# First pair's 32x32 systems of a delta-rule attention relaid on VectorE instead of over DRAM, and weight loads issued from ScalarE's queue

## The chip, the cores and the metric

The kernel runs on one NeuronCore of a Trainium2 chip. Its engines are TensorE (PE; PEld is its weight load), VectorE (DVE), ScalarE (ACT), GpSimd (POOL) and SyncE (SP), which here only issues DMAs. Each engine works through its own instructions in program order and waits on semaphores. The metric is the device time of one execution in microseconds (us); the profiled execution gives the trace.

## The reference

The program computes three stages that feed each other. First a delta-rule attention over 4 batches x 8 heads, 768 steps, head size 48:

```
k_n = k / (norm(k) + 1e-6)
for t in range(S):
    y[:, :, t] = q_t @ state
    v_old = state^T k_t
    state = state + beta_t * outer(k_t, v_t - v_old)
```

Its output, as 3072 tokens x 384, goes through a first MoE layer, which has one expert with a rational activation: `h = x @ w_in` (384 -> 2048), `g = P(h) / Q(h)` with a cubic P and a quadratic Q, `g @ w_out` (2048 -> 384). That output goes through a second MoE: a gate, a greedy assignment of 3072 tokens to 8 experts of capacity 384 in the order of their logits, and per expert `relu(x @ w1) @ w2`. The weights `w_in` and `w_out` come as 64-bit floats and are decoded on the chip to 32-bit and split into two 16-bit halves.

## The kernel before, in words

The recurrence is rewritten in 12 chunks of 64 steps. For each chunk and each of its 32 heads a unit lower triangular 64x64 system, built from the Gram matrix of the chunk's keys, is inverted. It is cut into 2x2 blocks of 32x32; two chunks form a pair, so that a pair gives 128 systems of 32x32, one per partition. `gram_k` (L124) multiplies the keys on PE into PSUM (tile `tg`), copies them to SBUF (`ka`, L131) and writes them to DRAM (`dA`, L134). `subst` (L160) reads them back so that one system lies along one partition (L167, eight DMAs into `pmA`), scales them (L94 on ACT, L100 to L106 and L178 on DVE) and runs the substitution column by column. For the first pair it runs on DVE (L183, L184) and stops at 16x16 blocks (15 columns, flag `n16`); for the other pairs on POOL (L187, L188, 31 columns). The result `pmW` goes to DRAM (`dW`, L190) and is read back transposed: for the first pair by `inv_in` (L157), for others by `diag_in` (L202). For the first pair `parts` (L153, L154) also reads the off-diagonal blocks of the Gram matrix back from `dA`, and `merge` (L1109) joins the 16x16 inverses to 32x32 with two PE products (L148), a transposition (L1115) and a subtraction (L1118) per chunk. Then the blocks are joined to 64x64 (`comb` L216, `comb2` L229), and the chunk's update follows: `tr` (L250), `y` (L264), `ds` (L272). The chunk's output is rounded to two 16-bit halves (`xs`, L1375 on ACT and L1376 on DVE) and laid out for the MoE by six DMAs (`pack`, L1380, tile `xT`).

The first MoE takes eight units per chunk, 96 in all. A unit is 18 matmuls (`h`, L875), the rational function on ACT and DVE (L848 to L868), a split into halves (L840 on ACT, L841 on DVE or POOL), and 12 matmuls (L824).

Ahead of the first unit lies the prologue. It loads the weights (`w_in` in six loads of 1 MB, L317; `w_out` in sixteen of 384 KB, L325), decodes them on DVE (three instructions a piece, L312 to L314) and rounds them (L1133, L1134, L1137 on ACT, L1138 on DVE, L1135 on POOL). All these loads are issued by SP, in one queue with the attention's transfers. The pieces of `w_out` that are not needed at once are decoded between the units of the first chunk.

The order of the instructions is set ahead of time by a list scheduler (`Sched`, L405). It gives each task an engine and a place by estimated costs and by due weights, which stand in the table `PP` (L967) for the prologue and the first two chunks and in `LP` (L1010) for the loop over chunks 2 to 10; two more tables serve the last chunk and the second MoE. Where it sees PE idle in the prologue it puts in matmuls on zeros (`warm`, L1395), 542 of them in all, which keep PE active. DMAs take eight semaphores in turn, so each DMA waits until the one eight places before it has landed.

Of the kernel before, what the change touches and what calls it, by code (L numbers as in the profile page):

```python
# [22 lines left out]
class Att:  # L23
# [11 lines left out]
    def __init__(s,ctx,tc,q,k,v,beta,tg,rec):  # L35
# [114 lines left out]
    def parts(s,m,e,F,X):  # L150
        nc=s.nc; x=s.dA[m%2][e]
        for h in range(2):
            for b in range(2): o=64*h+32*b; nc.sync.dma_start(F[o+16:o+32,:,0:16],x[o+16:o+32,:,32*b:32*b+16])  # L153
            nc.sync.dma_start(X[64*h:64*h+32],x[64*h:64*h+32,:,32:64])  # L154
    def inv_in(s,m,e,D):
        for h in range(2):
            for b in range(2): o=64*h+32*b; s.nc.sync.dma_start(D[o:o+32],s.dW[m%2][h,b,e].rearrange("u j i -> j u i"))  # L157

    def subst(s,m,eng,n16=False):

        nc=s.nc; n=128; x={}; ss=s.ss[m%2]; z=[]
# [7 lines left out]
        z+=[lambda: load(0),lambda: load(1)]  # L169
# [20 lines left out]
        z.append(lambda: (nc.sync if n16 else nc.gpsimd).dma_start(s.dW[m%2].rearrange("h b c u j i -> (h b c u) (j i)"),x['W'][:,0:1024]))  # L190
# [94 lines left out]
class Moe:  # L285
# [35 lines left out]
    def dma_wo(s,f):  # L321
# [3 lines left out]
        s.nc.sync.dma_start(ti,s.w_out.bitcast(I32).rearrange("(f p) (d two) -> f p d two",p=128,two=2)[f])  # L325
# [1164 lines left out]
```

## Time and profile before

| | |
|---|---|
| time, median of 3 runs | 968.44 us (965.59 to 973.08) |
| the profiled execution's own time | 968.31 us, of which its span is 966.5 us |
| busy share of the span | PE 88%, DVE 80%, ACT 58%, POOL 42% |
| first MoE unit's first matmul (L875) | 110.69 us after the span's start |
| last MoE unit's first stage | 671.5 us |
| DMA traffic | 97.50 MB, mean 101 GB/s |

Times in rows are us from the span's start. The profile's page shows the span in 40 slices of 24.2 us; a digit is a busy share in tenths. In the chain of waits each piece is the work that released the next one.

### The profile page before, as it was taken

The numbers are of one execution on the slowest core, as the hardware profiler recorded it, in microseconds if no ns is written. First come the engines' busy times: TensorE is split into PE (matmuls) and PEld (weight loads), VectorE is DVE, ScalarE is ACT, GpSimd is POOL, SyncE is SP. The second block draws the span as 40 slices with busy tenths as digits, with TensorE's granted clock in tenths as the row PEclk, the third lists the DMA queues.
The fourth block names the chain that finished last, engine by engine and source line by source line (L and its number), as shares of the span: only waits on it lengthen the run. The fifth ranks groups of instructions, "written<-read, shape, count | busy, mean of one in ns | idle before, by whom it ended". The sixth has DMA issues, their size and how long they took to land.

```text
span 966.5 us, 30502 instructions
## 1 busy us (share of the span) xinstructions
PE 855.1 (88%) x12967; PEld 603.6 (62%) x12967; DVE 771.9 (80%) x1689; ACT 562.8 (58%) x1019; POOL 405.5 (42%) x596
## 2 busy tenths in 40 slices
PE   8967798698989997999899999986789889998996
PEld 6846576575767675767677666663565555555663
DVE  5654798887889988989898898876688988988930
ACT  2132477566778787888778787875226334443821
POOL 1025870785227853785587212201322304213611
PEclk9976899899999999999999999997899979999998
DMA  8886436220561153216141220100054305443700
GB/s 305 186 241 121 128 113 113 53 74 23 146 121 52 56 122 100 63 57 156 38 91 51 54 55 1 34 5 14 2 169 159 151 30 196 156 155 128 266 25 24
DMA packets 101512, 97.50 MB, mean 101 GB/s; under 512 B 78336, under 2 KB 86144, under 8 KB 98560
## 3 DMA queue, kind: packets, MB, share of 16 engines
q1 hardware_dynamic: 95280, 58.33, 24.3%
q0 software_dynamic: 6096, 37.23, 10.4%
q8 instruction: 101, 1.65, 0.8%
q14 instruction: 35, 0.29, 0.1%
HBM read 71.68 MB, written 18.87 MB: 94 GB/s over the span
## 4 chain that ended last, share of the span: by engine, by line
PE 32%; DVE 29%; ACT 11%; DMA 10%; issue 10%; POOL 4%; SPq 3%; POOLq 0%; DVEq 0%; ACTq 0%
PE ph L875 9%; PE eph L770 4%; PE px L824 4%; DVE q L864 3%; DVE w L867 3%; DVE w L868 3%; PE px L783 3%; PE px L1395 3%; DVE w L851 2%; ACT q L858 2%; DVE q L850 2%; DMA xg<-x2d,perm 2%; DVE w L852 2%; ACT w L861 2%; DMA w1f<-in_moe_w_dram,ix 2%
## 5 line engine op out<-in xcount | busy, mean ns | idle before, releaser
L875 PE MATMUL ph<-xT,wi 128*128 128x256 f16 x1656 | 202.7, 278 | 26.4 <-DVE w L851 24.1
L875 PEld LDWEIGHTS <-wi 128*128 128x128 f16 x1728 | 167.0, 100 | 71.5 <-DVE w L851 34.6
L824 PE MATMUL px<-wo,gg 128*128 128x392 f16 (+1 forms) x1116 | 203.5, 333 | 5.2 <-ACT gg L840 2.9
L824 PEld LDWEIGHTS <-gg 128*128 128x128 f16 x1116 | 106.4, 99 | 75.0 <-issue 5.0
L841 POOL TENSOR_TENSOR gg<-w,gg 128x512 f16<-128x512 f32 x59 | 70.5, 1194 | 181.8 <-ACT gg L840 139.4
L188 POOL TENSOR_TENSOR pmW<-pmW,pmT 128x31 f32<-128x31 f32 (+15 forms) x155 | 94.9, 612 | 11.1
L187 POOL TENSOR_TENSOR pmT<-pmW,pmA 128x31 f32<-128x31 f32 (+15 forms) x155 | 86.6, 559 | 11.4
L861 ACT ACTIVATE w<-ph,cf 128x512 f32<-128x512 f32 x88 | 68.2, 775 | 22.8 <-PE ph L875 20.3
L867 DVE TENSOR_TENSOR w<-w,ph 128x512 f32<-128x512 f32 x88 | 59.8, 681 | 22.4 <-ACT q L858 12.2
L852 DVE SCALAR_TENSOR_TENSOR w<-q,w 128x512 f32<-128x512 f32 x88 | 76.5, 869 | 1.3
L840 ACT ACTIVATE gg<-w 128x512 f16<-128x512 f32 x88 | 55.4, 630 | 37.8 <-DVE w L852 37.3
L864 DVE SCALAR_TENSOR_TENSOR q<-q,cf,ph 128x512 f32<-128x512 f32 x88 | 65.1, 740 | 12.4 <-ACT w L861 6.8
L858 ACT ACTIVATE q<-ph,cf 128x512 f32<-128x512 f32 x88 | 60.0, 682 | 23.3 <-PE ph L875 12.7
L783 PEld LDWEIGHTS <-rr 128*128 128x128 f16 x576 | 52.3, 97 | 33.6 <-issue 2.3
L868 DVE SCALAR_TENSOR_TENSOR w<-w,cf,ph 128x512 f32<-128x512 f32 x88 | 65.3, 742 | 9.9 <-ACT q L858 9.4
L1395 PEld LDWEIGHTS <-warm 128*128 128x128 f16 x542 | 54.1, 104 | 24.5 <-issue 10.5
L773 ACT ACTIVATE rr<-eph 128x384 f16<-128x384 f32 x64 | 31.0, 490 | 60.3 <-PE eph L770 52.4
L850 DVE SCALAR_TENSOR_TENSOR q<-q,ph 128x512 f32<-128x512 f32 x88 | 59.8, 680 | 6.9 <-ACT ph L849 6.4
L865 ACT ACTIVATE q<-q 128x512 f32<-128x512 f32 x88 | 55.2, 628 | 16.9 <-DVE q L864 15.9
L851 DVE SCALAR_TENSOR_TENSOR w<-w,cf,ph 128x512 f32<-128x512 f32 x88 | 65.0, 738 | 0.0
L848 ACT ACTIVATE ph<-q,cf 128x512 f32<-128x512 f32 x88 | 60.6, 688 | 6.4 <-DVE ss L103 2.8
L788 POOL DMA_INDIRECT out_dram<-yo,perm x24 | 28.1, 1170 | 81.9 <-ACT yo L785 75.0
(342 smaller groups left out, 1649.7 us busy)
## 6 DMA issues: line engine op xcount, KB each, us to landing
kt<-in_k_dram SPq DMA_DIRECT2D x12, 512.0 KB, 4.0
dA<-ka SPq DMA_DIRECT2D x11, 512.0 KB, 3.6
vn<-in_v_dram SPq DMA_DIRECT2D x12, 384.0 KB, 4.7
qt<-in_q_dram SPq DMA_DIRECT2D x24, 192.0 KB, 4.1
kn<-in_k_dram SPq DMA_DIRECT2D x12, 384.0 KB, 3.1
x2d<-xr SPq DMA_DIRECT2D x44, 96.0 KB, 2.4
xT<-xs SPq DMA_DIRECT2D x24, 144.0 KB, 3.0
wst<-in_moe_w_out_dram SPq DMA_DIRECT2D x8, 384.0 KB, 3.8
```

The costliest lines, as they stand in the source:

```text
L187: if half==0: eng.tensor_tensor(t,W[:,0:r,j:j+1].to_broadcast([n,r,k]),A[:,j:j+1,j+1:32].to_broadcast([n,r,k]),op=OP.mult)
L188: else: eng.tensor_tensor(W[:,0:r,j+1:32],W[:,0:r,j+1:32],t,op=OP.subtract)
L783: g.add(('PE',.163,lambda P=P,rh=rh,wh=wh,f=f,part=part,i=i: nc.tensor.matmul(P,r[:,rh,f,128*i:128*i+128],W2[:,wh,f],start=(f,part)==(0,0) ...
L824: te.matmul(T['px',un//8][bp][:,0:O.N],gg()[:,gh,i,128*bp:128*bp+128],M.wo[:,wh,fb,0:O.N],start=fb==0 and n==0,stop=fb==15 and n==2,skip_g ...
L851: add(('DVE',.07+.6*z,lambda: ve.scalar_tensor_tensor(w(),w(),cf[:,0:1],y(),op0=OP.add,op1=OP.mult)),W+Y,W,un+O.pd('w3',un))
L852: add(('DVE*',.07+.535*z,lambda: ve.scalar_tensor_tensor(w(),q(),2.0,w(),op0=OP.subtract,op1=OP.mult)),Q+W,W,un+O.pd('w4',un))
L861: ac.activation(w(),P(),AF.Identity,bias=cf[:,2:3],scale=cf[:,3:4])
L864: add(('DVE',.07+.6*z,lambda: ve.scalar_tensor_tensor(q(),q(),cf[:,4:5],P(),op0=OP.add,op1=OP.mult)),Q+Pn,Q,un+O.pd('mu',un))
L867: add(('DVE',.07+.535*z,lambda: ve.tensor_tensor(w(),w(),P(),op=OP.mult)),W+Pn,W,un+O.pd('w1',un))
L868: add(('DVE',.07+.6*z,lambda: ve.scalar_tensor_tensor(w(),w(),cf[:,1:2],P(),op0=OP.add,op1=OP.mult)),W+Pn,W,un+O.pd('w2',un))
L875: for wh,xh in ((0,0),(0,1),(1,0)): te.matmul(T['P',un][:,i],M.wi[:,wh,part,128*fb:128*fb+128],xT()[:,xh,part],start=n==0,stop=n==8); n+=1
L1395: for _ in range(n): nc.tensor.matmul((bk['px1'] if t is None else t)[:,0:256],warm[:,0:128],warm,start=True,stop=True)
```

## The change

The first pair no longer goes over DRAM. Its two Gram matrices are computed into two PSUM tiles (`rec` for chunk 1, `tg` for chunk 0). `gram_0` copies each in small pieces from PSUM: the four diagonal 32x32 blocks into one SBUF tile `G`, in an order in which one stream transposition on DVE (32x32 blocks) gives `pmA`; the off-diagonal 16-column blocks, masked by a constant `odd`, and the upper blocks straight into the tiles that `parts` filled. After the substitution a second stream transposition writes the inverses to a tile `nd`, where `inv_in` put them. So 31 DMAs on SP fall away (2 writes of `dA`, 8 reads into `pmA`, 12 of `parts`, 1 write of `dW`, 8 of `inv_in`). The 6 loads of `w_in` and 16 of `w_out` are issued by ACT's queue instead of SP's. All due weights in `PP` and `LP` are new, so the order of the prologue and of the loop is another one. In the instruction lists, the matmuls on zeros become 406, five of the 88 whole splits at L841 go from POOL to DVE, and two copies at L1202 from DVE to ACT. From the last chunk on, the order of each engine stays the same.

```diff
+        s.odd=c.tile([128,1],F32,name="odd"); nc.vector.tensor_reduce(s.odd,s.ident.rearrange("t (a b x) -> t a b x",b=2,x=16)[:,:,1],axis=AX.XY,op=OP.add)
...
+    def gram_0(s,c,P,F):
+        nc=s.nc; k=s.kT[c]; g=s.gram(k,k,0,s.rec if c else s.tg)
+        def out(i,act=True):
+            o=slice(32*i,32*i+32); b=32*(i%2); y=s.G.rearrange("t (x c p r) -> t c r p x",x=32,c=2,p=8)[o,c]; x=g[o,:,:,b:b+32]
+            if act: nc.scalar.activation(y,x,AF.Copy)
+            else: nc.vector.tensor_copy(y,x)
+        def off(i): o=slice(32*i,32*i+32); b=32*(i%2); nc.scalar.activation(F[o].rearrange("t (p r) x -> t r p x",r=2)[:,:,:,0:16],g[o,:,:,b:b+16],AF.Copy,scale=s.odd[o])
+        def top(h): o=slice(64*h,64*h+32); nc.scalar.activation(P[o].rearrange("t (p r) x -> t r p x",r=2),g[o,:,:,32:64],AF.Copy)
...
-    def parts(s,m,e,F,X):
-        nc=s.nc; x=s.dA[m%2][e]
...
-    def inv_in(s,m,e,D):
...
-    def subst(s,m,eng,n16=False):
+    def subst(s,m,eng,n16=False,D=None):
...
-        z+=[lambda: load(0),lambda: load(1)]
+        def sys():
+            load(None); nc.vector.transpose(x['A'][:,0:1024],s.G)
+        z+=[sys] if n16 else [lambda: load(0),lambda: load(1)]
...
-        z.append(lambda: (nc.sync if n16 else nc.gpsimd).dma_start(s.dW[m%2].rearrange("h b c u j i -> (h b c u) (j i)"),x['W'][:,0:1024]))
+        if n16: z.append(lambda: nc.vector.transpose(D.rearrange("p (n i) -> p i n",i=32),x['W'][:,0:1024].rearrange("p (j i) -> p i j",i=32)))
+        else: z.append(lambda: nc.gpsimd.dma_start(s.dW[m%2].rearrange("h b c u j i -> (h b c u) (j i)"),x['W'][:,0:1024]))
...
-        s.nc.sync.dma_start(ti,s.w_out.bitcast(I32).rearrange("(f p) (d two) -> f p d two",p=128,two=2)[f])
+        s.nc.scalar.dma_start(ti,s.w_out.bitcast(I32).rearrange("(f p) (d two) -> f p d two",p=128,two=2)[f])
...
-PP=dict(K=[7339.93,4085.14,1736.19,-2114.71,1742.45,2256.15,42.43,5191.74,-1312.5],
+PP=dict(K=[2081.9,2098.33,2116.11,2982.83,-3313.15,1372.22,2452.84,-1832.06,-2116.3],
...
+    def GK0(c):
+        x=CH[c]; f,pp=x['F'],x['P']; p=PW('gk',c); B_=RE if c else TG
+        add(('POOL',.7,lambda: po.memset(flat(f),0.0)),[],[f],PP['ms'])
+        b=mm(2.4,warm(lambda: A.gram_0(c,sl(pp),sl(f))),['rec' if c else 'tg'],[('kT',c)],B_,p,act=2800)
+        for i in range(4): ev(b,i,'AD',.55,B_,[('g0',c,i)]+['ka'][:c==i==0],p)
+        for i in range(4): ev(b,4+i,'ACT',.4,B_,[f],p+1)
+        for h in range(2): ev(b,8+h,'ACT',.55,B_,[pp],p+2)
...
-        add(('SP',(6,1.2),lambda: A.parts(0,c,sl(f),sl(pp))),[('dA',0,c)],[f,pp],p)
-        add(('SP',(4,1.2),lambda: A.inv_in(0,c,sl(d))),[('dW',0)],[d],p)
...
-        hf,j=divmod(k,3); add(('SP',(1,2.9),lambda: M.dma_wi(k,sp,wsi[k])),[],WS_(k),PP['wil'][k])
+        hf,j=divmod(k,3); add(('SP',(1,2.9),lambda: M.dma_wi(k,ac,wsi[k])),[],WS_(k),PP['wil'][k])
```

The order moves at three places that matter below. In the order's rows a line number of the changed kernel is its own. The first place is SP's queue behind the small loads, of the kernel before (`dA`, `pmA`, `ut`, `n` belong to the first pair, `wsi` and `wst` to the weights):

```order
L134 DMA dA_116<-ka 128x1024
L317 DMA wsi<-in_moe_w_in_dram 128x2048
L134 DMA dA_117<-xs 128x1024
L325 DMA wst<-in_moe_w_out_dram 128x768
L89 DMA vn_96<-in_v_dram 128x768
L92 DMA qt_94<-in_q_dram 48x1024 x2
L325 DMA wst<-in_moe_w_out_dram 128x768
L167 DMA pmA<-dA_116 16x32x32 x4
L167 DMA pmA<-dA_117 16x32x32 x4
L317 DMA wsi<-in_moe_w_in_dram 128x2048
```

and of the changed kernel, where `dA` and `pmA` already belong to the second pair:

```order
L86 DMA kt_90<-in_k_dram 128x1024
L88 DMA kn_92<-in_k_dram 128x768
L88 DMA kn_93<-in_k_dram 128x768
L90 DMA vn_97<-in_v_dram 128x768
L145 DMA dA_120<-ka 128x1024
L169 DMA pmA<-dA_120 16x32x32 x4
L145 DMA dA_121<-ka 128x1024
L169 DMA pmA<-dA_121 16x32x32 x4
```

The loads of inputs stand ahead of everything that waits for an engine, and no weight load stands between them.

The second place is DVE ahead of the first pair's substitution, in the changed kernel (`ka` is the tile `G`, `q` and `wof` are weights being decoded):

```order
L130 COPY ka<-tg 32x2x8x32 x2
L317 TENSOR_SCALAR q<-wo 128x512
L172 STREAM_TRANSPOSE pmA<-ka 128x1024
L318 SCALAR_TENSOR_TENSOR q<-wo,q 128x512
L317 TENSOR_SCALAR q<-wo 128x512
L319 SCALAR_TENSOR_TENSOR q<-wo,q 128x512
L318 SCALAR_TENSOR_TENSOR q<-wo,q 128x512
L101 TENSOR_TENSOR ss_103<-pmA,ss_103 128x32
L319 SCALAR_TENSOR_TENSOR q<-wo,q 128x512
L1151 SCALAR_TENSOR_TENSOR wi<-q,wi 128x512
L102 SCALAR_TENSOR_TENSOR ss_103<-ss_103 128x32
```

Before, L100 to L106 followed each other on DVE with nothing between them, behind ten decoding instructions; now decoding stands between the relaying, the scaling and the substitution.

The third place is ACT at the same time in the changed kernel (`n` and `ut` are the tiles of `merge`):

```order
L129 ACTIVATE ka<-rec 32x2x8x32 x2
L330 DMA wst<-in_moe_w_out_dram 128x768
L131 ACTIVATE n_207<-rec,odd 32x2x8x16
L132 ACTIVATE n_206<-rec 32x2x8x32
L1150 ACTIVATE wo<-wof 128x384
L330 DMA wst<-in_moe_w_out_dram 128x768
L129 ACTIVATE ka<-tg 32x2x8x32
L330 DMA gg<-in_moe_w_out_dram 128x768
L129 ACTIVATE ka<-tg 32x2x8x32
L131 ACTIVATE ut<-tg,odd 32x2x8x16
L330 DMA gg<-in_moe_w_out_dram 128x768
L132 ACTIVATE ut<-tg 32x2x8x32
```

Before, ACT issued no DMA and took one copy per Gram matrix (L131); now loads stand between the pieces that it copies, each behind its own wait.

## Rows read from the trace of the kernel before

**Rows 1.** The page: busy us and shares; DMA's busy tenths in 40 slices.
```profile
PE 855.1 (88%) x12967; PEld 603.6 (62%) x12967; DVE 771.9 (80%) x1689; ACT 562.8 (58%) x1019; POOL 405.5 (42%) x596
...
DMA  8886436220561153216141220100054305443700
```

**Rows 2.** Windows: stretch, busy us per engine, PE's granted clock, DMA share, GB/s.
```profile
0.00:12.00 12.00, 8.68 (x68) 6.32 (x69) 5.92 (x13) 1.49 (x2) 2.94 (x11) 1.00 0.85 325
12.00:36.00 24.00, 24.00 (x308) 20.72 (x308) 12.77 (x31) 7.98 (x15) 0.73 (x3) 1.00 0.92 230
...
49.40:104.00 54.60, 38.62 (x1197) 29.80 (x1198) 32.16 (x59) 18.05 (x30) 24.95 (x33) 0.72 0.70 180
...
110.70:204.00 93.30, 81.07 (x1615) 62.53 (x1613) 76.84 (x138) 61.90 (x112) 55.72 (x85) 0.93 0.38 87
204.00:390.00 186.00, 168.60 (x3187) 124.16 (x3186) 160.22 (x243) 138.72 (x234) 102.40 (x172) 0.99 0.36 87
...
671.00:966.50 295.50, 263.37 (x2127) 162.01 (x2126) 223.85 (x799) 118.23 (x266) 82.57 (x113) 0.95 0.33 120
```

**Rows 3.** Chain of waits, 0 to 140 us: start, us, what.
```profile
18.69 8.55 DMA vn<-in_v_dram
...
31.46 6.78 DMA wsi<-in_moe_w_in_dram
...
38.63 9.26 DMA wo<-in_moe_w_in_dram
...
48.28 6.12 DMA kt<-in_k_dram
```

**Rows 4.** Timeline, prologue: start, us, engine, line, operation, tiles [idle before, releaser].
```profile
11.23 0.46 PE L121 MATMUL tg<-kt 48*64 48x64 f32 x16
...
16.66 29.98 PE L1395 MATMUL px<-warm 128*128 128x256 f16 x273
...
21.90 9.46 SPq L167 DMA_DIRECT2D pmA<-dA  x8
...
36.04 0.21 DVE L100 TENSOR_TENSOR ss<-pmA,ss 128x32 f32<-128x32 f32 x1 [7.01 <-ACT ss L94]
...
49.18 0.21 DVE L184 TENSOR_TENSOR pmW<-pmW,pmT 128x30 f32<-128x30 f32 x1
...
51.30 0.68 DVE L313 SCALAR_TENSOR_TENSOR y<-wsi,y 128x512 int32<-128x512 int32 x1
...
66.28 0.71 DVE L1115 STREAM_TRANSPOSE wo<-wo 128x512 f32<-128x512 f32 x1 [3.04 <-DMA wo<-dW]
...
101.33 1.09 DVE L314 SCALAR_TENSOR_TENSOR wo<-wsi,wo 128x512 int32<-128x512 int32 x1
...
104.02 1.21 DVE L1376 SCALAR_TENSOR_TENSOR xs<-rec,xs 128x1024 f16<-128x1024 f32 x1
...
110.69 4.09 PE L875 MATMUL ph<-xT,wi 128*128 128x256 f16 x36
```

**Rows 5.** One line's instructions: ns min/median/max, first and last start, forms.
```profile
L173 DVE STREAM_TRANSPOSE nt<-ss x6: 199/202/211, 37.7 to 468.6; 128x32 f32<-128x32 f32 x6
...
L232 ACT ACTIVATE tt<-rec x18: 570/580/590, 92.3 to 579.6; 32x512 f32<-32x512 f32 x18
...
L841 DVE TENSOR_TENSOR gg<-w,gg x29: 675/681/1600, 124.1 to 632.7; 128x512 f16<-128x512 f32 x29
...
L1202 DVE COPY xrt<-tg x5: 557/558/558, 145.8 to 213.2; 128x768 f16<-128x768 f16 x5
```

**Rows 6.** DMA, 0 to 113 us: packets, bytes, rate, small packets.
```profile
DMA packets 25826, 23.19 MB, mean 205 GB/s; under 512 B 20528, under 2 KB 21040, under 8 KB 25040
```

**Rows 7.** Timeline: the second pair's substitution on POOL, and its result.
```profile
92.50 0.24 POOL L187 TENSOR_TENSOR pmT<-pmW,pmA 128x31 f32<-128x31 f32 x1
...
135.35 0.79 POOL L190 DMA_DIRECT2D dW<-pmW  x1
...
144.92 1.40 SPq L202 DMA_DIRECT2D tt<-dW  x2
```

More of the change, by code (lines that the diff above doesn't have):

```diff
@@ L122, in gram, with gram_k @@
         return g
-    def gram_k(s,c,ka=None):
+    def gram_0(s,c,P,F):
[6 more added lines that the diff above has]
+        def top(h): o=slice(64*h,64*h+32); nc.scalar.activation(P[o].rearrange("t (p r) x -> t r p x",r=2),g[o,:,:,32:64],AF.Copy)
+        s.pend+=[lambda act=True,i=i: out(i,act) for i in range(4)]+[lambda i=i: off(i) for i in range(4)]+[lambda h=h: top(h) for h in range(2)]
+    def gram_k(s,c):
         nc=s.nc; k=s.kT[c%4]
         g=s.gram(k,k,0)
-        t=[ka]
+        t=[None]
         def out(act=True):
-            if ka is None: t[0]=s.wk.tile([128,U,64],F32,name="ka")
+            t[0]=s.wk.tile([128,U,64],F32,name="ka")
             o=t[0].rearrange("t (p r) x -> t r p x",r=2)
@@ L163, in load @@
             if not x: x.update(A=s.wk.tile([128,1056],F32,name="pmA"),W=s.wk.tile([128,1056],F32,name="pmW"),T=s.wk.tile([128,256],F32,name="pmT"))
-            for h in range(2):
+            for h in range(2) if c is not None else ():
                 for b in range(2):
@@ L1002 @@
     ux=1,
[L1003 to L1005 removed]
+    tol=0.3,
+    wg=1251.49,
+    wgf=-4090.52,
     wgb=0,
@@ L1086, in sub_pair @@
     def sub_pair(m,pr):
-        n16=m==0; e,en=(ve,'DVE*') if n16 else (po,'POOL*'); z=A.subst(m,e,n16); X=[('pm',0),('pm',1)]; S=('ss',m%2); K=15 if n16 else 31; f=(lambda n: dv(n)+.03) if n16 else pc
-        for c in range(2): add(('SP',(4,1.5),z[c]),[('dA',m%2,c)],[X[c]],pr)
+        n16=m==0; e,en=(ve,'DVE*') if n16 else (po,'POOL*'); z=A.subst(m,e,n16,T.get('nd')); z=z[:1]+z if n16 else z; X=[('pm',0),('pm',1)]; S=('ss',m%2); K=15 if n16 else 31; f=(lambda n: dv(n)+.03) if n16 else pc
+        if n16: add(('DVE',1.4,z[1]),[('g0',c,i) for c in range(2) for i in range(4)]+['ka'],X,pr)
+        for c in range(0 if n16 else 2): add(('SP',(4,1.5),z[c]),[('dA',m%2,c)],[X[c]],pr)
         add(('ACT',.25,z[2]),X,[S],pr)
@@ L1096, in sub_pair @@
             for h in range(2): add((en,d,z[12+2*j+h]),X,X,pr,chain=PP['pch'])
-        add(('SP',(1,1.5),z[12+2*K]) if n16 else ('POOL',1.1,z[12+2*K]),X,[('dW',m%2)],pr,post=0.0 if n16 else 3.0)
+        if n16: add(('DVE',1.4,z[12+2*K]),X,['nd0','nd1'],pr)
+        else: add(('POOL',1.1,z[12+2*K]),X,[('dW',m%2)],pr,post=3.0)
     add(('POOL',1.6,lambda: po.memset(A.TT,0.0)),[],TD,PP['ms'])
@@ L1119, in prologue, with tn @@
     c0=PP['c0'][0]
-    GK(0); GK(1); sub_pair(0,PP['c0'][0]); merge(0)
-    def tn(): t=A.st[0,'tn']=A.wk.tile([128,U,32],F32,name="tn"); ve.transpose(t,sl('h4'))
-    add(('DVE',.7,tn),['h4'],['tn'],c0)
+    GK0(0); GK0(1); sub_pair(0,PP['c0'][0]); merge(0)
+    def tn(): t=A.st[0,'tn']=A.wk.tile([128,U,32],F32,name="tn"); ve.transpose(t,sl('nd0'))
+    add(('DVE',.7,tn),['nd0'],['tn'],c0)
     def ttd(k,e):
-        o=32*k; c=o%64; y=lambda: A.TT[o:o+32,:,c:c+32]; x=lambda: sl('h4')[o:o+32]
+        o=32*k; c=o%64; y=lambda: A.TT[o:o+32,:,c:c+32]; x=lambda: sl('nd0')[o:o+32]
         return (lambda: ac.activation(y(),x(),AF.Copy)) if e=='ACT' else (lambda: po.tensor_copy(y(),x()))
-    for k in (1,3,0,2): add([('ACT',.55,ttd(k,'ACT')),('POOL',1.0,ttd(k,'POOL'))],['h4'],[('TT',k)],c0)
+    for k in (1,3,0,2): add([('ACT',.55,ttd(k,'ACT')),('POOL',1.0,ttd(k,'POOL'))],['nd0'],[('TT',k)],c0)
     def a12(): A.st[0,'A12']=sl('Ut1'); A.comb(0)
```

141 lines of the change are left out of this document (67 added, 74 removed).

## The prediction, made before the changed kernel ran

> **What bounds the kernel now.** I read the page's first two parts first: PE and DVE are the busiest engines, and DMA is at eight tenths or more in the first three slices and falls to six tenths or less later [rows 1]. Then the windows by stage, because shares of the whole span mix stages. From 110.7 to 204 us DVE is busy for 82% and PE for 87%, from 204 to 390 us for 86 and 91% [rows 2], both on the same repeated unit of the first MoE: throughput, little waiting. Ahead of it the picture is another one. In 49.4 to 104 us DVE works 32.2 of 54.6 us, ACT 18.1, POOL 25.0, and PE's 38.6 us contain many matmuls on zeros; its granted clock there is 0.72, a mixture of the two levels 1.2 and 2.4 GHz [rows 2]. So the prologue waits. The chain of waits says for what: landings of DMAs that stand one behind the other in SP's queue, 8.55, 6.78, 9.26 and 6.12 us [rows 3]. The timeline shows the first pair's path through them: its Gram matrix starts at 11.23, its eight reads occupy SP from 21.90 for 9.46 us, the substitution starts at 36.04 and ends at 49.39, the transposed inverse is there at 66.28 after DRAM, the first chunk's output is rounded at 104.02, and the first unit's matmul starts at 110.69 [rows 4]. Everything behind is a chain of units in fixed order, so what the prologue saves is carried to the end, less work that is only pushed behind the first unit.
>
> **The change part by part.** I follow the first pair through the new order.
>
> *Up to the relaid systems.* The first Gram matrix starts as before, at 11.4 (one small reduction is added on DVE). It takes about 2.3 us: 64 matmuls at 0.46 us for 16, and four on zeros at 0.11 (29.98 us for 273) [rows 4]. Thirty matmuls on zeros follow (3.3 us), then the second Gram matrix: it ends at 19.3. ACT copies the pieces. A piece of 32 partitions x 512 out of PSUM takes 0.58 us [rows 5]; the half-size ones lie between nothing and that, and I take 0.55 as a mean with the weight conversions among them. Thirteen such instructions and two DMA issues, each at most the 0.70 us that an issue took on SP (two in 1.40 [rows 7]), bring ACT from 13.7 to 22.3; two more pieces with an issue between them, to 24.2. The stream transposition of 1024 elements does not occur before. 32 elements take 0.20 us [rows 5] and 512 take 0.71 [rows 4]; a straight line gives 1.25, twice the larger 1.42. I take 1.3; the second, strided one could reach double that, 2.6, which I keep for the range. ACT's square root follows after eight more pieces and one issue (5 us), at 29.3. The substitution starts at 29 to 30 instead of 36.04: **about 7 us gained**.
>
> *The substitution* takes the 13.35 us that it took [rows 4], plus decoding that now stands inside: four instructions, three of them of the 0.68 us kind [rows 4], and constants, 2.9 us together. It ends at 45.5. Before, it ended at 49.39, so 4 us are left of the 7, but that decoding is no longer to be done later.
>
> *From there to the rounded first output.* Before: 54.6 us with 59 DVE instructions, 32.2 us busy, 0.545 us each [rows 2]; 22.4 us were idle, mostly for the writes and reads of the inverse, whose place was behind other loads. In the new order 53 instructions of the same kinds stand in this stretch: 28.9 us, 29.5 with the larger transposition. The path beside it (two products per chunk on PE, copies on ACT, joining) is shorter by my count at each step, so DVE's work sets the pace. POOL's substitution of the second pair runs beside the last third, and there a decoding instruction of 0.68 us took 1.09 [rows 4]; this is in the mean, since it was so before too. I add 2 us for waits that stay. The rounding (L1376) then starts at 77 instead of 104.02: **27 us gained**. All of it is idle time and a few instructions less, no faster instruction.
>
> *To the first unit* 6.67 us as before (104.02 to 110.69 [rows 4]): 83.7.
>
> *What comes back.* In the new order five DVE conversion instructions fewer stand ahead of the first unit; they are done later, on an engine that is at 82% there [rows 2]: 4 at 0.68 and one at 0.69 or less, 3.4 us. Five splits go from POOL to DVE at 0.68 us, two copies leave it at 0.56 [rows 5]: 2.3 us. Together **5.7 us lost** if DVE has no idle time to take them, nothing if it has; I take the full sum, since DVE bounds there.
>
> *At nothing:* the fewer matmuls on zeros, because they fill PE's idle time; the cover is that PE is not last in the new prologue. If it were, the 136 that fall away would be worth 15 us at 0.11. The moved loads cost ACT 22 issues, at most 15 us, of which ACT has 36 idle in the 54.6 us alone [rows 2].
>
> **Sum:** 968.3 (the profiled execution; the median is 968.4) - 27 + 5.7 = **947 us**. The order of chunks 2 to 10 is drawn anew too; its instructions are the same, so I count zero, with 2% of the 467 us from 204 to 671 either way, 9 us, for the range. The last 295 us [rows 2] keep their order.
>
> **The rivals.**
>
> *Transfers bind, whichever queue issues them.* Up to 113 us 23.19 MB were moved at a mean of 205 GB/s [rows 6], with the DMA engines 85 to 92% busy in the first 36 us [rows 2]. The change takes about 2.9 MB off (three writes of 0.5 MB; reads of 0.5, 0.5 and 0.4 MB). At 205 GB/s the 20.3 MB left need 99 us, and the first unit would start near 100: a gain of 10.7 - 5.7 = 5, **963 us**. Against it: 325 GB/s were reached in the first 12 us [rows 2], with which the same bytes need 62 us, and 20528 of the 25826 packets had under 512 B [rows 6], of which the removed reads made 12288 (1.4 MB in runs of 64 or 128 B). The Trainium skill, page "DMA: Bandwidth & Descriptors", section "Issuing engines are not separate DMA queues", speaks for this rival: DMAs of all issuing engines run on the same 16 DMA engines, and issuing from several only saves the issuing engine's own time. The rows here show one issuing queue only, so they don't yet decide it.
>
> *Loads block ACT (the other side).* A load on ACT's queue waits until the DMA eight places earlier has landed, and what ACT has to copy stands behind it. On SP such landings held the chain for 6.1 to 9.3 us, 7.7 in the mean [rows 3]. Four of the thirteen loads that now stand ahead of the first unit, held that long in front of a piece on the path, cost 31 us: 947 + 31 = **978 us**, slower. It decides from three on (23 us eat the gain). For it: the scheduler still books these loads on SP, so it does not see them hold ACT. Against: at ACT's first loads the DMAs eight places earlier are plain loads, issued without waiting for an engine.
>
> *The second pair on POOL comes late.* Its 42.9 us (92.50 to 135.35) and their use at 144.92 lie 34 us behind the first unit [rows 4, 7]. Now POOL would start near 70, with three conversions inside: result at 117 and landed at 120 or later, its use due at 118. A stall of 2 to 7 us, **952 us**.
>
> *The change doesn't do what it says:* the systems are there early, but the first unit still waits for converted weights; half of the 27 us, **960 us**.
>
> **How the numbers follow.** Chances: the sum as worked out 0.55 (its own range 940 to 955); the loop's order better by 2% 0.10 (938); POOL late 0.12; transfers 0.12; first unit held by weights 0.06; ACT blocked 0.05. Predicted is the likeliest, 947. Low end 932: the loop's 9 us better and the 5.7 us taken up by idle time. High end 963: transfers bind. Above it and below it I leave out the blocked ACT and about as much again below. About 1% is what a measurement of this kernel can tell from no change: 958.8 to 978. Faster: forecast, loop, POOL, and a third of the 960 case with some slack, 0.80; within 1%: 0.14; slower: 0.06.
>
> **What would show it.** Right: in the changed trace the square root at L95 near 29 us, the second stream transposition near 47, DVE with under 6 us idle from there to the rounding, the first MoE matmul at 80 to 88, then distances between units as before. Wrong: DVE waiting on weight loads in the first 60 us (transfers), ACT idle behind a DMA's issue with its input long ready (ACT), or SP or DVE waiting for `dW` near 118 (POOL). If the first unit comes at 84 and the end is not 20 us earlier, the new order behind it took the rest.

## The result, and the profile after

The changed kernel took 944.54 us (median of 4, 939.48 to 944.88) beside 969.88 us (965.59 to 973.08) before: ratio 0.9729, 95% interval 0.9677 to 0.9781. The profiled execution took 944.82 us, its span is 942.9. The forecast was 947 us, so the number was right; where the 26 us come from was not what the forecast said, and that is what the experiments are about.

The page of the changed kernel, busy us and shares, DMA's tenths, two queues (queue, packets, MB, share), answers [rows 1]:

```profile
PE 840.9 (89%) x12831; PEld 597.0 (63%) x12831; DVE 785.3 (83%) x1698; ACT 573.8 (61%) x1037; POOL 403.5 (43%) x590
...
DMA  8556415232453053405322120100054315444600
...
q10 hardware_dynamic: 3168, 12.58, 4.0%
q8 instruction: 100, 1.64, 0.8%
```

VectorE does 13.4 us more work than before, in a span 23.6 us shorter: only idle time fell away. Windows of the changed kernel (columns as in [rows 2]): from 12 to 36 us, the stretch from the end of the substitution to the first rounding (where before had 54.60 us with 32.16 us of VectorE [rows 2]), and the stretch from chunk 1 to the first MoE's last half unit.

```profile
12.00:36.00 24.00, 22.07 (x324) 17.66 (x327) 16.36 (x32) 16.76 (x29) 2.23 (x5) 0.93 0.76 255
47.23:85.29 38.06, 25.92 (x935) 20.78 (x935) 30.23 (x53) 13.74 (x23) 11.72 (x14) 0.65 0.60 147
...
175.20:657.40 482.20, 445.52 (x7853) 327.38 (x7852) 424.16 (x646) 372.50 (x629) 249.92 (x372) 0.98 0.27 68
```

The timeline of VectorE in the changed kernel, where [rows 4] had the way from the substitution to the rounding (the square root is ACT's, at 30.65):

```profile
26.93 1.24 DVE L172 STREAM_TRANSPOSE pmA<-ka 128x1024 f32<-128x1024 f32 x1
...
31.02 0.21 DVE L101 TENSOR_TENSOR ss<-pmA,ss 128x32 f32<-128x32 f32 x1 [0.73 <-ACT ss L95]
...
47.74 1.91 DVE L194 STREAM_TRANSPOSE nd<-pmW 128x1024 f32<-128x1024 f32 x1
...
58.91 0.69 DVE L1131 TENSOR_TENSOR nd<-nd,px 128x512 f32<-128x512 f32 x1 [1.38 <-PE px L159]
...
61.99 0.43 DVE L317 TENSOR_SCALAR w<-wsi 128x512 int32<-128x512 int32 x1 [0.48 <-DMA wsi<-in_moe_w_in_dram]
...
64.73 0.69 DVE L1131 TENSOR_TENSOR nd<-nd,ph 128x512 f32<-128x512 f32 x1 [2.31 <-PE ph L159]
...
75.03 0.69 DVE L238 TENSOR_SCALAR tt<-rec 32x512 f32<-32x512 f32 x1 [3.53 <-ACT tt L237]
...
85.29 1.23 DVE L1389 SCALAR_TENSOR_TENSOR xs<-rec,xs 128x1024 f16<-128x1024 f32 x1
```

VectorE's idle time in that stretch fell from 22.4 to 7.8 us. Of what is left, 3.7 us wait for two of TensorE's products, 3.5 for ScalarE's copy of a later product, 0.5 for a weight load. Before, the inverse's trip was not the greater part of it. Behind the row at 66.28, where the transposed inverse is there [rows 4], 12.7 of the 22.4 us wait for a weight load, for the second pair's square root and for ScalarE's copy. Ahead of it 6.22 us end at a weight load and 3.04 at the inverse's landing; the inverse was on its way during the 6.22 too, so these ends alone don't give the trip's price:

```profile
58.20 0.76 DVE L312 TENSOR_SCALAR w<-sbd 128x512 int32<-128x512 int32 x2 [6.22 <-DMA sbd<-in_moe_w_in_dram]
...
75.49 0.43 DVE L312 TENSOR_SCALAR wo<-wsi 128x512 int32<-128x512 int32 x1 [3.59 <-DMA wsi<-in_moe_w_in_dram]
...
83.45 0.21 DVE L100 TENSOR_TENSOR ss<-pmA,ss 128x32 f32<-128x32 f32 x1 [3.54 <-ACT ss L94]
...
92.95 0.69 DVE L233 TENSOR_SCALAR tt<-rec 32x512 f32<-32x512 f32 x1 [5.58 <-ACT tt L232]
```

The first rounding is 18.7 us earlier (85.29 for 104.02), the first unit 18.3 (92.39 for 110.69).

The table has one profiled execution of each kernel, in us: the square root, the end of the first substitution, the first rounding, the first MoE matmul, the start of chunk 1 (the ninth instruction of line L869, before L864), the first MoE's last half unit (that line's 97th and last instruction), the span; and the ratio of times to before.

```
                            root  subst   round  unit    chunk1  lastu   span   ratio (95%)
before                      35.7  49.4   104.0  110.7   180.6   675.6   966.5  1
changed                     30.7  47.2    85.3   92.4   175.2   657.4   942.9  0.9729 (0.9677-0.9781)
e1  old loop table          29.7  46.3    85.2   91.7   177.5   679.6   962.4  0.9934 (0.9910-0.9958)
e2  old prologue table      25.2  43.2    97.1  103.4   245.3   727.5  1013.4  1.0517 (1.0478-1.0556)
e3  before, both new tables 51.0  67.2   112.8  119.2   195.8   723.4  1011.0  1.0446 (1.0406-1.0485)
e4  weights on SP           28.2  45.0    83.6   92.0   174.8   653.2   938.3  0.9752 (0.9712-0.9792)
e5  second relay over DRAM  29.6  46.2    94.1  100.3   183.9   665.7   952.7  0.9785 (0.9753-0.9818)
e6  first relay over DRAM   31.3  48.3    86.7   93.8   176.6   655.1   941.4  0.9743 (0.9709-0.9777)
e7  copies in runs          28.0  44.6    83.3   89.5   176.1   654.9   941.8  0.9748 (0.9677-0.9818)
e8  narrow zero matmuls     29.8  46.4    85.7   92.7   176.4   664.1   948.5  0.9769 (0.9731-0.9807)
e9  before, new loop table  34.7  48.4   103.5  110.7   179.0   668.1   955.8  0.9906 (0.9869-0.9944)
e10 both relays over DRAM   31.5  48.6    96.5  103.6   183.5   665.4   951.4  0.9837 (0.9786-0.9889)
e11 fewer zero matmuls      30.6  47.2    88.4   95.8   174.2   655.6   943.2  0.9770 (0.9709-0.9832)
e12 late ones only, and e7  27.9  44.5    83.4   90.5   172.7   651.2   940.0  0.9757 (0.9726-0.9788)
```

The column `lastu` is where the expectations below say "the last chunk". It lies 40 to 43 us later than that chunk's start, which is at 635.2 us before and at 617.3 in the changed kernel (e12's expectation calls it chunk 10); the chunk itself takes 40.4 and 40.1 us, so the comparisons hold. The stretch behind `lastu` has one order in all of them and took 282.8 to 290.9 us: differences of some us between single spans say nothing, and the table's ratios carry the verdicts. The stretch from chunk 1 to `lastu` scatters as well: 478.4 to 487.7 us in the changed kernel, e4, e5, e6, e7 and e8, which have one order there. The profiled executions of e1, e3, e5 and e8 were their kernels' slowest runs.

The lead of the changed kernel is 18.3 us at the first unit, 5.4 at chunk 1 and 18.2 at the last half unit. So 13 us are given back between the first unit and chunk 1, and 13 are won in chunks 1 to 11, nearly all of them ahead of the last chunk, where the forecast counted zero.

### The profile page after: what moved, and what is told of

It reads as the page before. It is cut to its first block, busy times and chain, and to the rows that moved or that the text cites. A ratio compares the mean times of both kernels' runs of the same rounds, so it can differ in the third digit from the quotient of the medians.

```text
span 942.9 us, 30204 instructions
## 1 busy us (share of the span) xinstructions
PE 840.9 (89%) x12831; PEld 597.0 (63%) x12831; DVE 785.3 (83%) x1698; ACT 573.8 (61%) x1037; POOL 403.5 (43%) x590
## 3 DMA queue, kind: packets, MB, share of 16 engines
q8 instruction: 100, 1.64, 0.8%
## 4 chain that ended last, share of the span: by engine, by line
PE 33%; DVE 30%; ACT 14%; issue 11%; DMA 8%; POOL 3%; SPq 1%; ACTq 0%; POOLq 0%; DVEq 0%
PE ph L880 9%; PE eph L775 6%; PE px L829 4%; DVE q L869 4%; DVE w L872 4%; PE px L788 3%; ACT q L863 3%; DVE w L873 3%; ACT w L866 3%; DVE w L856 2%; DMA xg<-x2d,perm 2%; DVE q L855 2%; DMA qt<-in_q_dram 1%; DVE w L857 1%; PE tg L1408 1%
## 5 line engine op out<-in xcount | busy, mean ns | idle before, releaser
L846 POOL TENSOR_TENSOR gg<-w,gg 128x512 f16<-128x512 f32 x54 | 63.6, 1177 | 164.7 <-ACT gg L845 133.4
L191 POOL TENSOR_TENSOR pmT<-pmW,pmA 128x31 f32<-128x31 f32 (+15 forms) x155 | 90.3, 583 | 11.4
L857 DVE SCALAR_TENSOR_TENSOR w<-q,w 128x512 f32<-128x512 f32 x88 | 73.9, 841 | 1.2
L869 DVE SCALAR_TENSOR_TENSOR q<-q,cf,ph 128x512 f32<-128x512 f32 x88 | 65.3, 742 | 5.8 <-ACT w L866 5.1
L1408 PEld LDWEIGHTS <-warm 128*128 128x128 f16 x406 | 41.6, 107 | 23.5 <-issue 10.8
```

Source lines behind the costliest of these rows:

```text
L191: if half==0: eng.tensor_tensor(t,W[:,0:r,j:j+1].to_broadcast([n,r,k]),A[:,j:j+1,j+1:32].to_broadcast([n,r,k]),op=OP.mult)
L857: add(('DVE*',.07+.535*z,lambda: ve.scalar_tensor_tensor(w(),q(),2.0,w(),op0=OP.subtract,op1=OP.mult)),Q+W,W,un+O.pd('w4',un))
L869: add(('DVE',.07+.6*z,lambda: ve.scalar_tensor_tensor(q(),q(),cf[:,4:5],P(),op0=OP.add,op1=OP.mult)),Q+Pn,Q,un+O.pd('mu',un))
```

## The experiments

**e1: the changed kernel with the loop's old table.**

```diff
-LP=dict(tol=0.02, GP=9, f1=1428.36, ...
+LP=dict(tol=0.15, GP=9, f1=-1470.7, ...
```

> The changed kernel with the loop's old table of numbers (LP of before), all else as changed. Theory: the lead that the new relays give at the first unit (18 us) partly comes back in chunk 0, and some 12.5 us of the end result come from the loop's new order: from the start of chunk 1 to the last chunk the changed kernel took 482.2 us, the one before 495.0. Then the first unit still starts at 92 to 93 us, that stretch takes 490 to 498 us again, and the time is 952 to 960 us. Rival: the chunks are shorter because of what the prologue left behind (fewer conversions, other buffers), not because of their order: the stretch stays at 480 to 485 us and the time at 942 to 947 us.

959.57 us, as the theory had it. The first unit stays at 91.7 us, and the stretch from chunk 1 to `lastu` takes 502.1 us, more than the 490 to 498 of the theory. Of the whole gain 0.66% is left. The windows of that stretch, before, then e1:

```profile
180.60:675.60 495.00, 448.21 (x7850) 326.39 (x7849) 423.71 (x642) 373.12 (x630) 253.05 (x375) 0.97 0.27 66
```

```profile
177.50:679.60 502.10, 449.95 (x7849) 327.09 (x7848) 421.83 (x643) 372.04 (x626) 254.54 (x377) 0.97 0.28 65
```

VectorE is busy for 423.7, 421.8 and, in the changed kernel, 424.2 us: the same work in 495.0, 502.1 and 482.2 us. The loop's order is worth 20 us to the changed prologue, by the ratios too (0.9934 and 0.9729).

**e2: the changed kernel with the prologue's old table. e3: the kernel before with both new tables.**

```diff
-PP=dict(K=[2081.9,2098.33, ...
+PP=dict(K=[7339.93,4085.14, ...
```

> The changed kernel with the prologue's old table of numbers (PP of before), which was drawn for the order with the trips over DRAM; the relays on VectorE, the weights on ScalarE's queue and the new loop order stay. Theory: the chain of the first pair (Gram, relay, substitution, relay, products) sets the first unit, whatever the table: the root is at 30 to 32 us as in the change, but conversions stand in other places on VectorE, and the rounding of the first output moves from 85 to 88 to 95 us; the time is 946 to 956 us. Rival: the table alone makes the lead (with the old one the rounding falls back to 100 us or later): 958 us or more.

> The kernel before with both new tables of numbers (prologue and loop), but with its relays over DRAM and its weights on SyncE's queue. Theory: the loop's table gives its 12.5 us here too, the trips over DRAM stay and with them the rounding of the first output at 100 us or later: 955 to 963 us. Rival: the relays themselves give only the 5.4 us of lead that were left at the start of chunk 1, and the tables the rest of the 25 us: 947 to 952 us.

1015.88 and 1010.02 us: far above what either theory gave. e2's root is the earliest of all (25.2), its rounding comes at 97.1, between theory and rival, and then chunk 0 takes 136.5 us. TensorE's timeline of e2 in chunk 0 shows why:

```profile
159.18 46.33 PE L1408 MATMUL tg<-warm 128*128 128x256 f16 x411 [1.51 <-DVE wo L1220]
```

The planner puts zero matmuls into the gaps that its plan has. With a table that wasn't drawn for these dependencies the plan has a gap of tens of us, the chip has none, and 411 zero matmuls stand ahead of work that is ready: ACT waits 45.4 us for the product behind them. In e3, 152 of them take 16.76 us at 206 us; its root is late as well (51.0 us), since SyncE issues the last reads of the systems only from 44.66 to 48.26. So these two runs price plans that don't fit the kernel, not an order, and they decide nothing on the tables. They do show that zero matmuls can cost their full time.

**e4: the weights' loads back on SyncE.**

```diff
-        s.nc.scalar.dma_start(ti,...
+        s.nc.sync.dma_start(ti,...
-        add(('SP',(1,2.9),lambda: M.dma_wi(k,ac,wsi[k])),...
+        add(('SP',(1,2.9),lambda: M.dma_wi(k,sp,wsi[k])),...
```

> The changed kernel with the loads of the first weights issued by SyncE again (two words of the source). Theory: which queue issues them matters little: first unit within 2 us of 92.4 us, time 941 to 949 us. Rival 1: on SyncE the loads wait behind its other issues for their buffers, or hold those up, and the first unit comes 5 us later or more: 950 us or more. Rival 2: on ScalarE's queue a load that waits for its buffer (1.85 us at 14.7 us) holds up ScalarE's copies of the Gram products, so SyncE is better: the root comes 1.5 us or more before 30.65 us and the time is 938 to 942 us.

941.40 us, ratio within the changed kernel's interval: the queue is worth nothing measurable at the end. Rival 2's place is real (in the changed kernel ACT stood 1.85 us until 18.75 behind a load, and e4's root is 2.5 us earlier), but the first unit is only 0.4 us earlier; the time lies in both ranges. The Trainium skill (page "DMA: Bandwidth & Descriptors", section "Issuing engines are not separate DMA queues") says that DMAs issued by several engines run on the same 16 DMA engines and that issuing from several saves only issue time. The two ratios (0.9752 and 0.9729) agree with that.

**e5, e6, e10: the relays over DRAM again, every engine's order kept.** The planner still books a transposition on VectorE; in its place the function issues DMAs. e5 has the first edit, e6 the second, e10 both. e6's trip is one write and four reads, where the kernel before took two and eight.

```diff
-        if n16: z.append(lambda: nc.vector.transpose(D..., x['W']...))
+        def inv():
+            nc.sync.dma_start(s.dW[m%2]..., x['W'][:,0:1024])
+            for e in range(2): ... nc.sync.dma_start(D[o:o+32,512*e:512*e+512]..., s.dW[m%2][h,b,e]...)
...
-            load(None); nc.vector.transpose(x['A'][:,0:1024],s.G)
+            load(None); nc.sync.dma_start(s.dG,s.G...)
+            for o in range(0,128,32): nc.sync.dma_start(f3(x['A'])[o:o+32],s.dG[o:o+32].rearrange("j s i -> s j i"))
```

> The changed kernel, every engine's order kept, but the inverses go over DRAM again: in the place of the second stream transposition SyncE writes W and reads both inverses back. In the kernel before, that trip took 16.9 us (49.39 to 66.28). Theory: VectorE sets the pace from the substitution to chunk 1 (busy 140 of 175 us), its next instruction waits for the inverse, and the order has nothing to put there: the first output's rounding comes 12 to 16 us after 85.3, chunk 1 as much after 175.2, and the time is 954 to 961 us. Rival: something else than VectorE (weights, GpSimd's chain, TensorE's products) holds the first units, so that a third or less of the delay is left at chunk 1: 945 to 950 us.

> The changed kernel, every engine's order kept, but the systems go over DRAM again: in the place of the first stream transposition SyncE writes the collected Gram tile and reads it back by systems. The copies into that tile are laid in runs of 32 as the DRAM read wants them. Theory: the trip costs 5 to 9 us at the root (30.65 becomes 36 to 40 us), and since VectorE has conversions behind the root that can't pass the waiting one, two thirds or more of it are left at the first rounding: 948 to 953 us. Rival: a start that is earlier or later by a few us is lost before the first unit (with the weights on SyncE the root came 2.5 us earlier and the first unit only 0.4 us): 941 to 946 us.

> The changed kernel, every engine's order kept, with both relays over DRAM (the two earlier edits together). Theory: of the relays on VectorE only the second reaches the end, since its trip holds VectorE 9 us where the order has nothing to fill in (first rounding 94.1 in place of 85.3), and a root that is 1 to 3 us later is lost before chunk 1: 947 to 954 us, so that some 15 to 20 of the 25 us remain without any relay on VectorE. Rival: the two add up, and with the first late the loads of the second collide with weights: 958 us or more.

948.56, 943.34 and 953.16 us. e5's delay is smaller than forecast (8.8 us at the rounding, not 12 to 16), but all of it is there at chunk 1 (8.6): the theory on VectorE holds, the price of the trip was wrong, and so the time is its rival's. By the ratios 5 us are left at the end, which e5 alone doesn't tell from none. e6's time is its rival's too, but the delay is not lost where the rival had it: against e7, which has the same copies, the root is 3.3 us later, the rounding 3.4, the first unit 4.3, chunk 1 0.5, and the time is the same. So it is lost between the first unit and chunk 1. e10 is where the theory had it: without any relay on VectorE the new kernel keeps 1.6% of its 2.7%. **The relays are worth some 10 us of the 26 (0.9837 against 0.9729; the intervals barely miss each other, which makes it 3 to 18 us by an estimate from them), about half of it or more the second one.** Against e4, e6, e7 and e12 (0.9743 to 0.9757) it is 8 to 9 us. The other 16 are the order and what e10 leaves as changed: the blocks that `parts` read back still come straight from PSUM. No run separates these two in the prologue.

Why was the trip so cheap? SyncE's queue before, from the inverse's write on:

```profile
48.28 0.43 SPq L85 DMA_DIRECT2D kt<-in_k_dram  x1
...
49.76 0.38 SPq L190 DMA_DIRECT2D dW<-pmW  x1
59.14 0.32 SPq L134 DMA_DIRECT2D dA<-ka  x1
60.93 3.55 SPq L157 DMA_DIRECT2D wo<-dW  x4
```

The reads stand behind a write of `ka` that SyncE holds until 59.14. That write waits 8.9 us for ACT's copy, and the copy for TensorE's Gram product of the second pair, which waits for keys that SyncE itself issued only at 48.28 (first SyncE's waits for that copy up to 145 us: in total, times, longest):

```profile
SPq L134 <- ACT ka L131: 19.8, 3, 8.9
...
54.53 0.70 PE L121 MATMUL tg<-kt 48*64 48x64 f32 x16 [7.90 <-DMA kt<-in_k_dram]
...
58.09 1.03 ACT L131 ACTIVATE ka<-tg 128x1024 f32<-128x1024 f32 x1 [22.09 <-PE tg L121]
```

In e5 nothing stands between: the reads are issued 2.65 us after the write, where before it took 11.17, and VectorE goes on 9.4 us after the substitution's end, not 16.9. From there to the rounding the stretch takes 47.9 us in e5, 54.6 before and 38.1 in the changed kernel: 6.7 of the 16.6 us come with the trip in place, 9.9 with the relay. SyncE, then VectorE in e5:

```profile
46.20 0.33 SPq L195 DMA_DIRECT2D dW<-pmW  x1
48.85 4.05 SPq L198 DMA_DIRECT2D nd<-dW  x8
...
55.59 0.71 DVE L1133 STREAM_TRANSPOSE qt<-nd 128x512 f32<-128x512 f32 x1 [8.10 <-DMA nd<-dW]
```

**e7: the copies of the Gram products in runs of 32.**

```diff
-            ... y=s.G.rearrange("t (x c p r) -> t c r p x",x=32,c=2,p=8)[o,c]; ...
+            ... y=s.G.rearrange("t (c p r x) -> t c r p x",x=32,c=2,p=8)[o,c]; ...
-            load(None); nc.vector.transpose(x['A'][:,0:1024],s.G)
+            load(None); nc.vector.transpose(f3(x['A']),s.G.rearrange("p (n i) -> p i n",i=32))
```

> The changed kernel with the copies of the Gram products written in runs of 32 elements, and the first stream transposition reading with a stride of 32 elements in their place (as the second one does). Theory: the scattered write makes the copies of 32x512 take 1.04 us where copies of as many elements in runs take 0.58; so now they take 0.55 to 0.62 us, the transposition 1.5 to 1.9 us in place of 1.24, and the root comes 0.8 to 2 us earlier; of that little reaches the end: 940 to 944 us. Rival: the price lies in the 32 partitions or in reading PSUM, not in the written stride: copies stay at 1.0 us and the root comes 0.3 to 0.6 us later.

942.67 us, no measurable difference to the changed kernel, as the theory had it. The copies and the transposition by line (ns min/median/max, starts, forms), the changed kernel, then e7:

```profile
L129 ACT ACTIVATE ka<-rec x3: 1045/1076/1084, 12.6 to 15.8; 32x512 f32<-32x512 f32 x3
...
L172 DVE STREAM_TRANSPOSE pmA<-ka x1: 1240/1240/1240, 26.9 to 26.9; 128x1024 f32<-128x1024 f32 x1
```

```profile
L129 ACT ACTIVATE ka<-rec x3: 587/590/590, 12.9 to 14.8; 32x512 f32<-32x512 f32 x3
...
L172 DVE STREAM_TRANSPOSE pmA<-ka x1: 1953/1953/1953, 24.3 to 24.3; 128x1024 f32<-128x1024 f32 x1
```

The scattered write is the price: 0.59 us in runs, 1.08 without. The transposition pays 0.71 us for its stride. The root comes 2.6 us earlier, more than the 2 of the theory, the first unit 2.9, chunk 1 is 0.9 later.

**e8: 92 zero matmuls of 128 columns at the start for 46 of 256.**

```diff
-            hot(H00)
+            for _ in range(2*H00): nc.tensor.matmul(bk['px1'][:,0:128],warm[:,0:128],warm[:,0:128],start=True,stop=True)
```

> The changed kernel with 92 zero matmuls of 128 columns at its start in place of 46 of 256 (the same columns, 92 instructions more in TensorE's stream: each matmul has its weight load). In the changed kernel TensorE stands 1.49 us after the 77th matmul of the third merge product and 3.33 us after the 71st of the fourth, though it waits for nothing that the profile shows; between the two lie 256 instructions. Theory: the stand comes every 256 instructions of the stream, as if the next block of instructions were not there yet; with 92 more ahead it comes 46 matmuls earlier in each product (after the 31st and the 25th). Rival: the product waits for data or a semaphore that isn't shown: it stands after the 77th and the 71st again. Time in both cases 940 to 948 us.

947.32 us, inside the range. TensorE's timeline, the merge products of the changed kernel, then those of e8:

```profile
55.86 0.85 PE L159 MATMUL px<-qt 32*32 32x32 f32 x77
58.20 0.64 PE L159 MATMUL px<-qt 32*32 32x32 f32 x51 [1.49 <-issue]
...
59.53 0.83 PE L159 MATMUL ph<-wo 32*32 32x32 f32 x71
63.69 1.01 PE L159 MATMUL ph<-wo 32*32 32x32 f32 x57 [3.33 <-issue]
```

```profile
54.67 0.45 PE L159 MATMUL px<-qt 32*32 32x32 f32 x31
56.30 1.02 PE L159 MATMUL px<-qt 32*32 32x32 f32 x97 [1.18 <-issue]
...
58.01 0.40 PE L159 MATMUL ph<-wo 32*32 32x32 f32 x25
62.60 1.43 PE L159 MATMUL ph<-wo 32*32 32x32 f32 x103 [4.18 <-issue]
```

The theory holds to the instruction: 77 became 31, 71 became 25. The stands belong to the instruction stream, not to data.

**e9: the kernel before with the loop's new table alone** (its `LP` replaced by the changed one).

> The kernel before with the loop's new table alone. With the changed prologue that table was worth about 19 us (its ratio to before went from 0.9934 to 0.973). Theory: it is worth as much on its own: the stretch from chunk 1 to the last chunk falls from 495 to 475 to 485 us and the time is 948 to 956 us, without any relay on VectorE. Rival: a loop's table fits only the prologue that it was drawn for (the old one took 495.0 us after the old prologue and 502.1 after the new one): the stretch stays at 490 us or goes above, 963 us or more.

958.10 us: between the two. The stretch from chunk 1 to `lastu` takes 489.1 us (495.0 before, 482.2 in the changed kernel). A window of e9 over that stretch:

```profile
179.00:668.10 489.10, 448.05 (x7848) 329.55 (x7848) 429.68 (x657) 368.89 (x623) 252.28 (x370) 0.97 0.27 67
```

Alone the table is worth 0.9% (9 us), the new prologue without it 0.7% (6 us, e1), both 2.7%. The two don't add: together they give more than their sum. That a loop order fits the prologue it was drawn for is a reading of this, not shown by itself.

**e11: at most 8 zero matmuls in a gap. e12: only from 90 us of the plan on, with e7's copies.**

```diff
+                    n=min(n+k,8)-k
                     if x is not None: hot(n+k,x); ...
```

> The changed kernel with at most 8 zero matmuls put into one gap of the plan (or the few more that the planner wants for the clock). In the changed kernel 30 of them (3.45 us) stand ahead of the second Gram product, and 29 (6.03 us at half clock) at 145 us ahead of a transposition for which ScalarE waits 5.98 and VectorE 6.32 us. Theory: they fill gaps that the plan sees and the chip doesn't have; without them the root comes 1 to 3 us earlier, that wait falls below 2.5 us, chunk 1 starts 3 to 6 us earlier and the time is 935 to 941 us. Rival: without them TensorE's granted clock falls to its lower level in more places, the products and units there take longer, and the time is 943 us or more.

> The changed kernel with at most 8 zero matmuls in a gap from 90 us of the plan on alone (18, 29 and 12 of them become 8), and with the copies of the Gram products in runs of 32. With the limit everywhere chunk 0 took 71.4 us in place of 75.5, but TensorE ran at its lower clock from 20 to 100 us and the first rounding came 3 us later. Theory: the early zero matmuls keep the clock, the late ones only stand in the way: the first rounding stays at 83 to 85.5 us, chunk 0 takes 70 to 73 us, chunk 1 starts at 170 to 173 us and the time is 935 to 940 us, 2 to 6 us under the changed kernel. Rival: what chunk 0 gives up comes back in chunks 1 to 3, whose order was drawn for the state that the prologue leaves: chunk 10 starts within 2 us of 617.3 and the time is 941 to 945 us.

946.08 us for e11. The theory is right on chunk 0 (71.4 us for 75.5), wrong on the root (30.6, no earlier), and its rival is right on the rest: from 20 to 100 us the granted clock falls, and the rounding comes 3.1 us later. The windows of that stretch, the changed kernel, then e11 (last but two: the clock):

```profile
20.00:100.00 80.00, 61.39 (x1577) 50.29 (x1574) 64.56 (x129) 33.07 (x58) 28.55 (x39) 0.74 0.60 177
```

```profile
20.00:100.00 80.00, 46.25 (x1385) 35.49 (x1389) 62.02 (x128) 31.66 (x56) 26.02 (x35) 0.59 0.55 171
```

942.36 us for e12: the rounding stays (83.4), chunk 0 takes 72.0 us, chunk 1 starts 2.5 us earlier and the last half unit 6.2 (against e7, which has the same copies, 3.4 and 3.7), but the time isn't told apart from the changed kernel's or from e7's 942.67. So the theory's time failed, and the rival's reason for it, a loss in chunks 1 to 3, isn't seen either. At 145 us, TensorE of the changed kernel and VectorE behind it, then TensorE of e12:

```profile
145.13 6.03 PE L1408 MATMUL tg<-warm 128*128 128x256 f16 x29 [4.84 <-DVE wo L1220]
150.99 0.50 PE L388 MATMUL tg<-id,wo 128*128 128x128 f16 x6
...
154.36 0.17 DVE L1220 SCALAR_TENSOR_TENSOR wo<-tg,wo 128x8 f16<-128x8 f32 x1 [6.32 <-ACT wo L1219]
```

```profile
144.90 1.55 PE L1409 MATMUL tg<-warm 128*128 128x256 f16 x8 [4.76 <-DVE wo L1220]
146.25 0.85 PE L388 MATMUL tg<-id,wo 128*128 128x128 f16 x6
```

Here 29 zero matmuls hold a transposition for 4.5 us longer than 8 do; ACT's wait for it falls from 5.98 to 1.80 us and VectorE's behind it from 6.32 to 3.46.

## Why the prediction was right or wrong, point by point

- *Up to the root (forecast 29.3, 7 us gained):* 30.65 in the profile, 27.9 to 31.5 in the kernels that keep the changed prologue's table. The copies into `G` took 1.04 to 1.08 us, not 0.55, and ACT stood 1.85 us behind a load; the 30 zero matmuls ahead of the second Gram took 3.45, as counted. Of 5 us gained the relay itself gives 3.3 (e6 against e7).
- *The substitution (13.35 + 2.9 us):* 16.6 us from root to end, as forecast.
- *From there to the rounding (77, 27 us gained):* **this step failed twice.** It put most of VectorE's 22.4 idle us down to the inverse's trip over DRAM; it named the trip's place in the queue, but gave all of it to the relay. The rows of before show 3.3 of the 22.4 us ending at an inverse's landing and 9.8 at weight loads. e5, with the trip in place, shows that the trip costs 8.8 us at the rounding, and that 7.5 of the 16.9 us before were SyncE's queue, which the new order clears. And the prediction called the path beside VectorE shorter and added 2 us for waits that stay: they measured 7.8. Of these, 3.7 are waits for two of TensorE's products, which stood for 1.49 and 3.33 us in their own instruction stream. Of the 8.3 us by which the rounding is late, the waits make 5.8, the later end of the substitution 1.7, VectorE's work 0.7: its 53 instructions took 30.23 us (28.9 to 29.5 forecast), the strided transposition 1.91 us, inside its bounds of 1.3 and 2.6.
- *To the first unit, 6.67 us:* 7.1.
- *What comes back (5.7 us):* 13, so what the prologue saved was not carried on. 3.8 of them lie between the first unit's first matmul and VectorE's first instruction on it (7.3 us, before 3.6): TensorE turns to chunk 1's products after 12 of the unit's 36 matmuls.

```profile
92.39 2.74 PE L880 MATMUL ph<-xT,wi 128*128 128x256 f16 x12
...
97.47 2.79 PE L880 MATMUL ph<-xT,wi 128*128 128x256 f16 x24
```

  9.1 lie in chunk 0's units (windows before, then changed): VectorE has 6.9 us more to do, as forecast in kind, and is idle for 2.2 more.

```profile
114.20:180.60 66.40, 57.08 (x1227) 44.06 (x1225) 59.03 (x105) 44.39 (x79) 31.65 (x49) 0.97 0.43 96
```

```profile
99.70:175.20 75.50, 60.37 (x1073) 46.80 (x1071) 65.96 (x111) 45.89 (x81) 39.67 (x57) 0.93 0.35 81
```

  With fewer zero matmuls chunk 0 is 3.5 us shorter (e12), so "at nothing" was the wrong entry for them up to chunk 1: fewer in number, but one gap's 29 stand on the path. At the end e12 shows no time for it. That chunk 1 starts at 174.8 to 176.6 us whenever the rounding comes between 83.3 and 86.7 (changed, e4, e6, e7, e8) shows that a lead of 3 us ahead of it is lost there; what sets that floor is not settled.
- *The loop's order (0 ± 9):* 13 us gained against before, 20 against the old table behind the same prologue. This is the other mis-sized term. It was the forecast's rival with a chance of 0.10, and it made up for the 8 us of lead that the prologue lacked.
- *The rivals:* transfers don't bind (VectorE waited for weights 0.48 us between the substitution and the rounding; 255 GB/s from 12 to 36 us where 230 were moved before [rows 2]). Before, 9.8 us of its waits there ended at weight loads; no run separates which part of the new order took them away, but e4 shows that it isn't the issuing queue. ACT was held by a load, but for 1.85 us. GpSimd's inverses were written at 135.80, no earlier than before [rows 7], and no engine waited for them in chunk 0.

So the right number is luck in good part: 947 was reached by 8 us too much in the prologue, 7 too little in the give-back, and 13 to 18 that the sum had at zero: the loop's order, and 5 us in the last stretch that kernels of the same order there show in both directions.

## What to carry to other kernels

A wait at the end of a DRAM trip is not the price of the trip: look up in the issuing queue what stands between the write and the read, and what that waits for; here the trip took 16.9 us, and 9.4 with nothing in the queue between. When a change comes with a new order, keep the order and undo the change alone (put the old transfer into the same slot) before crediting it: that split 26 us into some 10 for the relays and 16 for what came along. The loop's order is worth 9 us to the kernel before and 20 behind the new prologue, so neither can be credited alone. Fillers that a plan places delay what stands behind them for their full time wherever the plan's gap isn't there on the chip (46.33 us in e2); whether that reaches the end is another question (not measurably in e12).

## What the runs showed of the hardware

- TensorE's instruction stream comes in blocks. In the third and fourth merge product it stands at two places 256 instructions apart (matmul and weight load counted apart): in the changed kernel, e6, e7 and e8 for 1.2 to 1.5 us, then for 3.3 to 4.4, in e5 for 4.99 and 0.42, at places that moved by exactly the instructions added in e8. The page's queue q8 moved 100 packets, 1.64 MB, for 2 x 12831 instructions, which is 100.2 blocks of 256. In the changed kernel's trace the packets of q8 at the two stands start at 55.43 and 60.29 us and take 1.56 and 1.95; TensorE stands from 56.71 to 58.20 and from 60.36 to 63.69, so it goes on 1.2 and 1.5 us after the packet's end, and the second packet starts only as TensorE stops. The Trainium skill (page "Runtime: NRT & Kernel Launch", section "Instruction fetch mechanics") says that a sequencer fetches its next 256 instructions by its own DMA queue while it runs the present ones, and that this is mostly hidden. The blocks agree; hidden it isn't in these products, which use up 256 instructions in about 2 us. What makes one block later than another wasn't tried.
- ScalarE's copy of 32x512 from PSUM takes 0.59 us in runs of 32 and 1.04 to 1.08 us when neighbouring elements are written 32 elements apart; VectorE's stream transposition of 128x1024 takes 1.24 us contiguous, 1.95 with a stride of 32 elements on its input (e7) and 1.91 with one on input and output.
